# A new hand-written order of all tasks in a fused attention and feed-forward kernel

## The chip, the core and the metric

The kernel runs on one core of one Trainium2 chip. The metric is device time of one execution in microseconds (us). The core has five engines with a queue of their own each: TensorE (PE, with its weight loads shown as PEld), VectorE (DVE), ScalarE (ACT), GpSimd (POOL) and SyncE (SP), which here only issues DMAs. Each engine takes its instructions strictly in the order in which the program holds them, and they wait for each other through semaphores.

## The reference

The input x has 2048 tokens of 512 features. Two branches read it, and a gate of one value per token mixes them:

```python
q, k, v = x @ wq, x @ wk, x @ wv             # 32 heads of 16, four segments of 512 tokens
for s in range(4):                           # memory attention, branch A
    p = softmax(qs @ ks.T * scale + mask)    # causal within the segment
    a_dot = p @ vs
    a_mem = (phi(qs) @ M) / (phi(qs) @ z + 1e-6)      # phi(t) = t + 1 if t > 0 else exp(t)
    o = sigmoid(beta) * a_mem + (1 - sigmoid(beta)) * a_dot
    M, z = M + phi(ks).T @ vs, z + phi(ks).sum(0)
a = concat(o) @ wo
b = (gelu(x @ w_gate) * (x @ w_up)) @ w_down # branch B, 1792 hidden features
g = sigmoid((x * gate_w).sum(-1))
out = g * a + (1 - g) * b
```

## The kernel before

Everything is in bf16 with sums in f32. x is kept transposed in SBUF (xT: four chunks of 128 features by 2048 tokens), the weights too. The work is cut into named tasks, each belonging to one engine. A task's function issues the instructions; the class `Sched` (lines 160 to 193) goes through the text `ORDER` (lines 32 to 144) word by word and calls them. So `ORDER` is the schedule of all five engines at once: an engine's queue is the sequence of its own tasks in that text. A word is a name, then after @ the engine (A, D, P for ACT, DVE, POOL) where a task may go to several, then after # the letters of the buffers that it takes.

The names that matter, with s for the segment and c for a block of eight heads:

- `q{s}.{c}`, `k{s}.{c}`, `v{s}.{kt}`, `up{s}.{h}`: projection groups on PE, 16 small matmuls each; `gt{s}.{h}` is a pair of gate groups. `e` ahead of the name is the task that empties the PSUM bank: copies on DVE or ACT, the gelu on ACT for `egt`, the product with the gelu on DVE for `eup`. There are two single banks ("gen") and three double ones ("lg").
- `lg{n}`, n from 0 to 79: a slot of logits on PE (line 643), into two lg banks; `ex{n}a`, `ex{n}b`: the exponentials on ACT (line 664); `as{n}a`, `as{n}b`: the causal masks on POOL (line 673). `pv{s}.{c}e` and `pv{s}.{c}o`: probabilities times v on PE (line 692), each reading the masks of three slots; `epv` transposes the result on DVE (line 710); then `r`, `rg`, `n`, `m`, `o` normalise, add the memory part and transpose back into xT.
- `Ek`, `Emk`, `Qk`, `phk` and the same with q: the feature map, an exponential on ACT, two elementwise steps on DVE and a sum on DVE or POOL (line 767). For k the sum goes to a buffer `pkT`, of which there is one; `pk{s}.{p}` then issues two DMA transposes on SP (line 796) from pkT to `pk`, which `M{s}.{p}` multiplies with v on PE (line 808).
- `ko{s}.{c}`: a copy of k with every other head kept (line 406), on DVE or POOL. `den`, `num`, `rma`, `rmr`, `rmg`, `nm`: the memory read-out.
- `z{s}.{kt}`: the gate's products on DVE (line 525), 16 of them, from copies of x that lie in the buffers of `wdn` and `wo`; `zsp`: copies of their sums on POOL (line 536). Only when these are read can the SP tasks `wdn` and `wo` load the weights into the same buffers. `wos0` to `wos3` scale wo in place.
- `lx2`, `lx3`: SP loads segments 2 and 3 of x by four DMA transposes each (line 290); segment 1 and all other loads are issued ahead of the ordered part (lines 306 to 322).
- `dn{s}.{qt}.{h}` and `wo{s}.{qt}.{c}`: the output groups on PE; `os`, `st`: the scaled copy and the store of 128 rows. The last group is cut in two halves (`3.3h0`, `3.3h1`).

What orders the SP queue around the change is the place of its words among the others:

```python
    TAB["wo"] = add("wo", "SP", lambda _: load_w(nc.sync, wo, A_wo), kind="wol",
                    deps=zs[3 * KT:])
    a_x = [None, ext("x1")] + [add(f"lx{s}", "SP", lambda _, s=s: load_x(s), kind="lx")
                               for s in range(2, NSEG)]
```

Of the kernel before, what the change touches and what calls it, by code (L numbers as in the profile page):

```python
# [35 lines left out]
k0f3.1 q0.0#aa ek0.3@A ek0.0@D ek0.2@D gt0.1#b ko0.0@P#a Ek0.1#a ek0.1@A gt0.0#a Emk0.1 ko0.1@D  # L36
Qk0.1#a ko0.2@D#b ko0.3@D q0.1#b phk0.1@D#a egt0.0#a gt0.5#c eq0.1@D eq0.0@A egt0.1#b q0.2#ab
egt0.5#c lg0#ab eq0.2@D v0.1#b gt0.3#c ex0a#a Ek0.0#a q1.0#ac pk0.1#a ex0b#b gt1.4#a eq1.0@D z0.0
gt0.2#b Qk0.0#a egt1.4#d z0.3 ev0.1@D egt0.3#e Emk0.0 up0.3#a phk0.0@P#a egt0.2#f v0.3#b eup0.3
lg1#ac ev0.3@D up0.1#a as0a z2.1 ex1a#c v0.0#b eup0.1 ex1b#d as1a lg2#ba ev0.0@D v1.2#a as0b z1.0  # L40
ex2a#e q1.1#b ev1.2@D ex2b#f as2a lg3#cb eq1.1@D v1.0#a as1b tb ex3a#g as2b up0.5#b ev1.0@D ex3b#h
z3.3 lg4#ac v0.2#a ex4a#i eup0.5 omg v1.3#b ex4b#j as4a eb lg5#ba Eq1.0#a ev0.2@D as4b gt0.4#c
ev1.3@D as3a ex5a#k as3b Emq1.0 z3.1 ex5b#l pv0.0e#aa z2.0 gt1.1#b Qq1.0#a z1.3 epv0.0e gt0.6#a
egt0.4#g z3.0 egt1.1#h z0.2 pv0.0o#b bde0@D z3.2 egt0.6#i k1.0#ac epv0.0o wo lg6#cb lx3 ek1.0@D
up1.8#b ex6b#a up0.11#a eup1.8 ex6a#b lg7#ab eup0.11 k1.1#b ex7a#c as6a q0.3#a ek1.1@D as5a ex7b#d
bde3@D lg8#ca phq1.0@D#a M0.1#b ex8a#e gt1.5#b z1.1 lx2 r0.0#a Ek1.0#a z1.2 z0.1 gt1.2#c ex8b#f
eq0.3@D eM0.1 z2.3 gt1.3#a z2.2 egt1.5#j ko1.0@D#c zsp2 Qk1.0#a Emk1.0 egt1.2#k gt1.6#b pk0.0#b
as8b as7b egt1.3#l as5b as6b up0.7#a egt1.6#m as7a up0.13#b eup0.7 zsp1 lg9#ca eup0.13 zsp0
pv0.1e#ab ex9b#g phk1.0@D#a q1.2#ba epv0.1e pk1.0#a ex9a#h as9b lg10#ba eq1.2@D k2.0#aa as8a
ex10a#i ko1.1@P up1.9#b ek2.0@D ex10b#j wdn lg11#cb eup1.9 v1.1#a as9a ex11a#a bde2@P pv0.1o#b  # L50
as10b ex11b#b ev1.1@D as11a lg12#ac epv0.1o up0.12#a ex12a#k zsp3 r0.1#b q1.3#b eup0.12 ex12b#l
lg13#ba eq1.3@D g2 up1.7#a ex13b#c M0.0#b ex13a#d lg14#ca as13b eM0.0 rg0.1 up0.4#b as11b eup1.7
ex14b#e as12b up1.2#a eup0.4 as10a ex14a#f as13a lg15#ba eup1.2 bde1@P up0.6#b ex15b#g as14b
n0.1#a gt2.2#c ex15a#h as15b eup0.6 as12a Eq1.1#a as14a up0.10#a Qq1.1#a gt1.0#a eup0.10 wos1@D
egt2.2#n mbd0.1 Emq1.1 omz pv0.2e#bb egt1.0#o up1.3#a epv0.2e phq1.1@D#b lg16#bc up0.2#b eup1.3
ex16a#a zbd0 up1.5#a rg0.0 mbd0.2 mbd0.0 eup0.2 ex16b#b lg17#ab eup1.5 k2.1#b ex17b#i pv0.2o#a
ek2.1@D ex17a#j lg18#cb epv0.2o up0.8#b ex18b#c r0.2#b rg0.2 M1.0#a ex18a#d eM1.0 lg19#ab eup0.8
q2.0#ab n0.2#b ex19a#e up1.12#b wos0@D eq2.0@D ex19b#f as19a lg20#ca as17b den1#aa ex20a#k gt2.0#b
eden1 eup1.12 ex20b#l as20a as16a gt2.1#c as15a rma1.0#a egt2.0#p gt2.3#a as18a egt2.1#q as17a
as16b up1.6#a as18b egt2.3#r rma1.2 pv0.3e#bb eup1.6 lg21#bc epv0.3e up1.11#a as19b ex21b#a wos3@P  # L60
up0.9#b eup1.11 ex21a#b lg22#ac eup0.9 up1.10#a as21b ex22b#g as20b pv0.3o#b eup1.10 rma1.1
ex22a#h lg23#bc epv0.3o up1.1#a ex23b#c as22b k1.2#bb eup1.1 as22a ex23a#d mbd0.3 lg24#ac rma1.3
ek1.2@D k1.3#a ex24b#e up0.0#b ek1.3@D ex24a#f as24b lg25#bc as23b o0.2 Ek1.1#a num1.0#aa as23a
gt2.5#a eup0.0 as21a ex25a#i n0.0#b as24a Qk1.1#a ex25b#j pv1.0e#ba ko1.2@P#a gt2.6#b rmr1 o0.0
Emk1.1 egt2.5#s gt2.4#c r0.3#b enum1.0 egt2.6#t epv1.0e phk1.1@D#a pv1.0o#a egt2.4#u up1.4#b rg0.3
pk1.1#b epv1.0o lg26#ab eup1.4 v2.2#a n0.3#b ex26b#a q2.1#b ev2.2@D ex26a#b rmg1 lg27#cb eq2.1@D
up2.10#a ex27b#k as26a up2.13#b eup2.10 ex27a#l as27b r1.0#a lg28#ab rg1.0 ko1.3@P v2.0#a eup2.13
ex28b#c o0.3 up1.13#b ex28a#d ev2.0@D lg29#cb eup1.13 Eq2.0#a up2.2#a as28a as28b as27a ex29a#e
up2.4#b eup2.2 as25b as26b ex29b#f lg30#ac eup2.4 up2.5#a as25a Qq2.0#a ex30b#g as29b pv1.1e#bb
eup2.5 as29a ex30a#h lg31#bc epv1.1e as30b up2.3#a ex31b#a pv1.1o#b eup2.3 ex31a#b lg32#ac epv1.1o  # L70
up2.7#a ex32b#i n1.0#b up2.8#b mbd1.0 eup2.7 ex32a#j as32b lg33#bc eup2.8 up2.11#a as31b ex33b#c
nm1.0@D#a as32a k2.2#bc ex33a#d eup2.11 as31a lg34#ac ek2.2@D num1.1#aa ex34b#e as33b enum1.1
v2.1#b as33a ex34a#f as34b lg35#bc ev2.1@D up2.1#a as30a ex35b#k as34a o0.1 pv1.2e#ba nm1.1@P#b
eup2.1 ex35a#l lg36#ac epv1.2e pv1.2o#a wos2@P ex36b#a up2.0#b epv1.2o ex36a#b lg37#bc eup2.0
k2.3#a ex37b#g Emq2.0 phq2.0@D#c up1.0#b ex37a#h as37b ek2.3@D lg38#ac m1.0@P eup1.0 q3.0#ac
ex38b#c r1.1#b mbd1.1 q3.1#b rg1.1 ex38a#d eq3.0@D as38b as36a r1.2#a lg39#bc eq3.1@A rg1.2
dn0.3.0#a as35a dn0.3.1 ex39b#e as36b dn0.3.2 dn0.3.3 v2.3#b as37a Ek2.0#a as39b dn0.3.4 dn0.3.5
ev2.3@D dn0.3.6 as35b ex39a#f dn0.3.7 Qk2.0#a lg40#ac n1.2#a dn0.3.8 ex40b#i dn0.3.9 dn0.3.10
Emk2.0 num1.2#ba phk2.0@D#a dn0.3.11 dn0.3.12 ex40a#j dn0.3.13 as40b enum1.2 wo0.3.0 pk2.0#a
wo0.3.1 as39a wo0.3.2 o1.0 wo0.3.3 pv1.3e#ba as38a os0.3@A#a ko2.0@D#b lg41#bc epv1.3e pv1.3o#a  # L80
ex41a#a up2.9#b epv1.3o ex41b#b as41a r1.3#a lg42#ab eup2.9 nm1.2@P#c q2.2#aa ex42b#k M1.1#b as40a
eq2.2@A lg43#cb eM1.1 Eq3.0#a num1.3#ba dn0.0.0#a dn0.0.1 enum1.3 dn0.0.2 dn0.0.3 ex43b#l dn0.0.4
Qq3.0#a dn0.0.5 Emq3.0 q2.3#b rg1.3 ex43a#c m1.2@D mbd1.3 dn0.0.6 o1.2 dn0.0.7 ex42a#d dn0.0.8
dn0.0.9 nm1.3@D#a lg44#bc dn0.0.10 eq2.3@D ex44a#e dn0.0.11 dn0.0.12 dn0.0.13 phq3.0@D#a dn0.2.0#b
ex44b#f wo0.0.0 n1.3#b lg45#ab dn0.2.1 m1.3@D wo0.0.1 Eq2.1#a dn0.2.2 o1.3 wo0.0.2 wo0.0.3 gt3.4#c
zbd1 ex45a#g os0.0@D#b Emq2.1 st0.0 ex45b#h Qq2.1#a phq2.1@D#b dn0.2.3 dn0.2.4 dn0.2.5 as45b
dn0.2.6 dn0.2.7 as43a dn0.1.0#a as42a dn0.1.1 dn0.2.8 dn0.2.9 egt3.4#a as41b dn0.2.10 dn0.2.11
dn0.2.12 as42b dn0.2.13 wo0.2.0 wo0.2.1 as44b wo0.2.2 wo0.2.3 as45a lg46#ab os0.2@D#c ko2.1@P
Ek2.1#a dn0.1.2 dn0.1.3 pv2.0e#ba Qk2.1#a gt3.0#c ex46a#a as44a epv2.0e Emk2.1 as46a M2.0#b
dn0.1.4 as43b dn0.1.5 eM2.0 phk2.1@D#a dn0.1.6 egt3.0#b den2#ba dn0.1.7 mbd1.2 dn0.1.8 pk2.1#b  # L90
eden2 dn0.1.9 dn0.1.10 dn0.1.11 ko2.2@D#c dn0.1.12 rma2.0#a dn0.1.13 n1.1#a wo0.1.0 wo0.1.1
wo0.1.2 ex46b#b ko2.3@D wo0.1.3 lg47#ac os0.1@D#d rma2.3 pv2.0o#b ex47a#i m1.1@D k3.0#ab st0.1
epv2.0o ex47b#j as47a lg48#ba ek3.0@D v3.0#b rma2.1 ex48b#c dn1.3.0#a dn1.3.1 ev3.0@D ex48a#d
lg49#ca as47b dn1.3.2 M2.1#b ex49a#e as46b dn1.3.3 dn1.3.4 eM2.1 r2.0#a rma2.2 pv2.1e#bb ex49b#f
lg50#bc epv2.1e dn1.3.5 ex50a#k dn1.3.6 as49b dn1.3.7 rmr2 dn1.3.8 dn1.3.9 as48b num2.1#ba ex50b#l
as49a lg51#ab enum2.1 dn1.3.10 as48a dn1.3.11 ex51a#a mbd2.1 dn1.3.12 dn1.3.13 rmg2 wo1.3.0 o1.1
nm2.1@P#c pv2.1o#b ex51b#b lg52#ca epv2.1o wo1.3.1 ex52b#g wo1.3.2 wo1.3.3 q3.2#bb os1.3@D#b
ex52a#h r2.1#b lg53#ba st1.3 eq3.2@D num2.0#aa ex53a#c st0.3 gt3.5#c enum2.0 st0.2 ex53b#d
nm2.0@D#a num2.3#ba lg54#ba enum2.3 up2.6#a ex54a#e rg2.1 n2.1#b k3.1#b ex54b#f mbd2.0 m2.1@P
eup2.6 gt3.6#b ek3.1@D as54a as52b egt3.5#f k3.2#aa as53a as51b up3.8#b egt3.6#e ek3.2@D as52a  # L100
# [939 lines left out]
```

## Time and profile before

| | |
|---|---|
| median of three runs | 277.04 us (277.0 to 278.11) |
| the profiled execution's own time | 279.19 us |
| its span, first to last instruction | 277.5 us |
| mean granted TensorE clock in it | 0.994 |
| busy share PE, ACT, DVE, POOL | 96%, 82%, 65%, 51% |
| bytes moved by DMA | 15.83 MB |

The page shows one execution. Its second part cuts the span into 40 equal slices of 6.9 us and gives each engine's busy share in tenths. A group row gives line, engine, operation, names and shape, the count, then busy us and the mean ns of one, then the idle time before them and who ended it. A row of the waits reads: engine and line that waited, the one that it waited for, us in total, times, longest. A row of a timeline or of the chain begins with the start in us and the duration; in brackets stands the idle time before it.

### The profile page before, as it was taken

The numbers are of one execution on the slowest core, as the hardware profiler recorded it, in microseconds if no ns is written. First come the engines' busy times: TensorE is split into PE (matmuls) and PEld (weight loads), VectorE is DVE, ScalarE is ACT, GpSimd is POOL, SyncE is SP. The second block draws the span as 40 slices with busy tenths as digits, with TensorE's granted clock in tenths as the row PEclk, the third lists the DMA queues.
The fourth block names the chain that finished last, engine by engine and source line by source line (L and its number), as shares of the span: only waits on it lengthen the run. The fifth ranks groups of instructions, "written<-read, shape, count | busy, mean of one in ns | idle before, by whom it ended". The sixth has DMA issues, their size and how long they took to land.

```text
span 277.5 us, 11576 instructions
## 1 busy us (share of the span) xinstructions
PE 266.9 (96%) x5219; PEld 132.7 (48%) x5220; DVE 180.1 (65%) x355; ACT 228.6 (82%) x261; POOL 140.9 (51%) x264
## 2 busy tenths in 40 slices
PE   8999999978999999999999999999999999999993
...
ACT  2589999993999999999999999989998999970000
...
PEclk9999999997999999999999999999999999999999
...
GB/s 223 361 254 306 55 4 100 95 79 169 138 2 2 2 2 5 40 4 2 2 2 41 21 2 59 6 59 2 2 2 4 2 2 2 40 6 2 78 21 79
DMA packets 23539, 15.83 MB, mean 57 GB/s; under 512 B 13761, under 2 KB 22465, under 8 KB 23489
## 3 DMA queue, kind: packets, MB, share of 16 engines
...
q8 instruction: 41, 0.67, 1.1%
...
q14 instruction: 10, 0.07, 0.1%
HBM read 9.84 MB, written 2.10 MB: 43 GB/s over the span
## 4 chain that ended last, share of the span: by engine, by line
PE 78%; DMA 6%; DVE 6%; SPq 4%; POOL 3%; issue 1%; ACT 0%; ACTq 0%; DVEq 0%; POOLq 0%
PE dn L377 22%; PE up L377 17%; PE gt L377 11%; PE lg L643 8%; PE pv L692 6%; PE v L377 5%; PE k L377 4%; SPq L290 3%; PE q L377 3%; DMA wdn<-in_gate_w_dram 3%; POOL pT L673 2%; DVE wdn L525 2%; POOL rm L873 1%; DMA wdn<-in_A_x_dram 1%; PE num L377 1%
## 5 line engine op out<-in xcount | busy, mean ns | idle before, releaser
L230 ACT ACTIVATE pT<-lg 128x1024 bf16<-128x1024 f32 x160 | 152.4, 1028 | 10.5 <-PE lg L643 9.3
L673 POOL TENSOR_SCALAR_AFFINE_SELECT pT<-pT 128x512 bf16<-128x512 bf16 (+1 forms) x160 | 85.2, 564 | 72.1 <-ACT pT L230 68.4
L377 PE MATMUL dn<-wdn,G 128*32 128x512 bf16 (+1 forms) x952 | 60.2, 367 | 0.1
L377 PE MATMUL up<-xT,wup 128*32 128x512 bf16 x896 | 57.4, 384 | 0.0
L573 DVE TENSOR_TENSOR G<-up,G 128x512 bf16<-128x512 f32 x56 | 38.4, 687 | 22.7 <-PE up L377 22.4
L377 PE MATMUL gt<-xT,wga 128*32 128x512 bf16 x800 | 46.0, 379 | 0.0
L377 PEld LDWEIGHTS <-G 128*32 128x32 bf16 x952 | 24.0, 96 | 21.0 <-issue 2.4
L377 PEld LDWEIGHTS <-wup 128*32 128x32 bf16 x896 | 22.6, 97 | 22.4 <-issue 4.3
L710 DVE STREAM_TRANSPOSE T<-pv 128x512 f32<-128x512 f32 x32 | 22.6, 709 | 15.1 <-PE pv L692 14.7
L377 PEld LDWEIGHTS <-wga 128*32 128x32 bf16 x800 | 21.7, 97 | 19.8 <-issue 0.4
L230 ACT ACTIVATE G<-gt 128x1024 bf16<-128x1024 f32 x28 | 27.4, 1017 | 1.5 <-PE gt L373 0.9
L228 ACT ACT_TABLE_LOAD x22 | 28.2, 1283 | 0.4
L692 PE MATMUL pv<-pT,vz 128*32 128x256 bf16 (+2 forms) x640 | 23.2, 273 | 0.4 <-POOL pT L673 0.4
L948 ACT ACTIVATE osb<-dn,omz 128x512 bf16<-128x512 f32 (+1 forms) x3 | 1.8, 616 | 24.0 <-PE dn L377 24.0
L692 PEld LDWEIGHTS <-vz 128*32 128x32 bf16 x640 | 14.9, 97 | 10.9 <-issue 1.2
L377 PE MATMUL dn<-wo,xT 128*32 128x512 bf16 (+1 forms) x272 | 19.3, 367 | 0.0
L377 PEld LDWEIGHTS <-xT 128*32 128x32 bf16 x528 | 12.8, 96 | 13.3 <-issue 3.3
L950 DVE TENSOR_SCALAR osb<-dn,omz 128x512 bf16<-128x512 f32 (+1 forms) x14 | 10.2, 727 | 12.3 <-PE dn L377 12.1
L643 PE MATMUL lg<-qT,kO 32*128 32x128 bf16 (+2 forms) x320 | 17.6, 272 | 0.0
L643 PE MATMUL lg<-qT,kT 16*128 16x256 bf16 (+2 forms) x320 | 17.5, 273 | 0.0
L377 PE MATMUL v<-wv,xT 128*32 128x512 bf16 x256 | 16.6, 381 | 0.8 <-DVE vz L236 0.6
L873 POOL TENSOR_SCALAR rm<-Tm 32x32 f32<-32x32 f32 x48 | 14.6, 304 | 4.9 <-DVE Tm L867 1.7
...
## 6 DMA issues: line engine op xcount, KB each, us to landing
...
```

What stands on the lines that cost most here:

```text
L228: nc.scalar.activation(nil[0][:, 1:2], nil[0][:, 0:1], func)
L230: nc.scalar.activation(dst, src, func, **kw)
L290: nc.sync.dma_start_transpose(xT[:, fc, s * L:(s + 1) * L], x2[s * L:(s + 1) * L, fc * P:(fc + 1) * P])
L377: nc.tensor.matmul(out[a], lhsT=lhsT[:, a], rhs=rhs, start=start, stop=stop, tile_position=(0, 32 * j), skip_group_check=True)
L525: nc.vector.scalar_tensor_tensor(out=xr[s][:, kt, :], in0=xr[s][:, kt, :], scalar=1.0, in1=gwb, op0=ALU.mult, op1=ALU.mult, accum_out=zc[: ...
L573: UPT[(s, hs)] = evac("DVE", g, box, lambda e, t: nc.vector.tensor_mul(G[(s, hs // 2)][:, hs % 2, :], t[:, :], G[(s, hs // 2)][:, hs % 2, ...
L643: nc.tensor.matmul(A[j // 2][:, j % 2, at * P:(at + nq) * P], lhsT=l, rhs=r, start=True, stop=True, tile_position=(32 * j, 0))
L673: nc.gpsimd.affine_select(out=v, in_=v, pattern=pat, compare_op=ALU.is_ge, fill=0.0, base=0, channel_multiplier=-1)
L692: nc.tensor.matmul(t[32 * j:32 * j + 32, qb * P:(qb + nq) * P], lhsT=vz[s % 2][:, kt, h * VW:h * VW + 32], rhs=pT[(s, t0 + w, j // 2)][:, ...
L710: nc.vector.transpose(TT[key][:, e, :, :].rearrange("p a b -> p (a b)"), t[:, :])
L873: eng_of[e].tensor_scalar_add(RMt[s][32 * j:32 * j + 32, c, :, :], bx["Td"][32 * c:32 * c + 32, :, 2 * j:2 * j + 2], 1e-6)
L950: nc.vector.tensor_scalar_mul(bx["o"][:, lo:hi], box["t"][:, 0:hi - lo], g)
```

## The change

Only the text `ORDER` is replaced from its fourth line on; no function changes. The same tasks are called in another sequence, some on another engine, some with other buffer letters. On SP the tasks stand as follows:

```
before: pk0.1 wo lx3 lx2 pk0.0 pk1.0 wdn pk1.1 pk2.0 st0.0 pk2.1 st0.1 st1.3 st0.3 st0.2 st1.2 ...
after:  pk0.0 lx2 pk0.1 pk1.0 lx3 wo pk1.1 wdn pk2.0 st0.3 pk2.1 st0.1 st1.3 st1.1 st1.0 st0.0 ...
```

Tasks by engine, where one can be chosen:

| | before | after |
|---|---|---|
| odd copies `ko` on POOL | 6 of 16 | 9 of 16 |
| feature sums `phk`, `phq` on POOL | 1 and 1 | 3 and 1 |
| memory products `nm` on POOL | 7 of 12 | 9 of 12 |
| `bde`, `wos` on POOL | 2 and 2 | 1 and 1 |
| copies `ek`, `eq`, `ev` on ACT | 3, 3, 0 | 5, 3, 1 |
| output copies `os` on ACT | 3 of 17 | 6 of 17 |
| changes between gelu and exponentials on ACT | 22 | 20 |

The core of the diff, the stretch from the first q group to lg9 (the rest is of the same kind):

```diff
-k0f3.1 q0.0#aa ek0.3@A ek0.0@D ek0.2@D gt0.1#b ko0.0@P#a Ek0.1#a ek0.1@A gt0.0#a Emk0.1 ko0.1@D
-Qk0.1#a ko0.2@D#b ko0.3@D q0.1#b phk0.1@D#a egt0.0#a gt0.5#c eq0.1@D eq0.0@A egt0.1#b q0.2#ab
-egt0.5#c lg0#ab eq0.2@D v0.1#b gt0.3#c ex0a#a Ek0.0#a q1.0#ac pk0.1#a ex0b#b gt1.4#a eq1.0@D z0.0
-gt0.2#b Qk0.0#a egt1.4#d z0.3 ev0.1@D egt0.3#e Emk0.0 up0.3#a phk0.0@P#a egt0.2#f v0.3#b eup0.3
...
-egt0.4#g z3.0 egt1.1#h z0.2 pv0.0o#b bde0@D z3.2 egt0.6#i k1.0#ac epv0.0o wo lg6#cb lx3 ek1.0@D
-up1.8#b ex6b#a up0.11#a eup1.8 ex6a#b lg7#ab eup0.11 k1.1#b ex7a#c as6a q0.3#a ek1.1@D as5a ex7b#d
-bde3@D lg8#ca phq1.0@D#a M0.1#b ex8a#e gt1.5#b z1.1 lx2 r0.0#a Ek1.0#a z1.2 z0.1 gt1.2#c ex8b#f
-eq0.3@D eM0.1 z2.3 gt1.3#a z2.2 egt1.5#j ko1.0@D#c zsp2 Qk1.0#a Emk1.0 egt1.2#k gt1.6#b pk0.0#b
-as8b as7b egt1.3#l as5b as6b up0.7#a egt1.6#m as7a up0.13#b eup0.7 zsp1 lg9#ca eup0.13 zsp0
-pv0.1e#ab ex9b#g phk1.0@D#a q1.2#ba epv0.1e pk1.0#a ex9a#h as9b lg10#ba eq1.2@D k2.0#aa as8a
...
+k0f3.1 q0.0#aa ek0.3@A ek0.0@D ek0.1@A gt0.1#b ko0.0@P#a ek0.2@A Ek0.0#a gt0.0#c Emk0.0 Qk0.0#a
+phk0.0@P#a egt0.1#a v0.1#b egt0.0#b gt0.2#a ev0.1@D ko0.2@P#b eq0.0@A lg0#bc egt0.2#c q0.1#b
+ko0.1@P v0.3#a eq0.1@D ko0.3@P gt0.5#a ev0.3@D ex0a#a Ek0.1#a q0.2#bb pk0.0#a ex0b#b gt1.4#b
+eq0.2@D gt0.3#c egt0.5#d egt1.4#e z0.3 q1.0#ac z0.1 egt0.3#f v1.0#b lx2 eq1.0@D lg1#ab ev1.0@D
+v1.2#a z1.3 ex1a#c up0.3#b ev1.2@D ex1b#d as1a lg2#ca eup0.3 up1.8#a Emk0.1 ex2b#e as1b q1.1#b
+eup1.8 tb ex2a#f as2b lg3#ba eq1.1@D up0.11#a ex3a#g Qk0.1#a phk0.1@D#a v0.0#b ex3b#h eup0.11
+pk0.1#b lg4#cb ev0.0@D v0.2#a ex4b#i up0.7#b ex4a#j ev0.2@D as4b lg5#ab as2a eup0.7 Eq1.0#a
+gt1.1#c as0a as3b ex5a#k as4a as0b M0.0#a ex5b#l as5a gt0.4#a eM0.0 as3a z1.0 Qq1.0#a M0.1#b
+gt0.6#b egt1.1#g eM0.1 Emq1.0 omg phq1.0@D#a pv0.0e#aa z1.1 egt0.6#i up0.5#b epv0.0e eb
+lg6#ca eup0.5 k1.0#ac ex6a#a k1.1#b ek1.0@D ex6b#b as6a lg7#bc ek1.1@D v1.1#a as5b bde1@D ex7a#c
+as6b up0.1#b ev1.1@D bde2@P ex7b#d z2.0 lg8#ab pv0.0o#a Ek1.0#a z3.1 gt1.3#c z2.1 ex8b#e epv0.0o
+ex8a#f r0.0#a gt1.6#b z0.0 z2.3 mbd0.1 z1.2 gt1.5#a egt1.6#j z3.0 eup0.1 egt1.3#k gt1.2#b Emk1.0
+z3.3 egt1.5#l z2.2 z3.2 up0.13#a egt1.2#m z0.2 up0.4#b eup0.13 zsp2 lg9#ca eup0.4 k2.0#aa as7a
+ex9b#g as8a up1.11#b ek2.0@D as7b ex9a#h as8b lg10#ba eup1.11 zsp0 q1.2#aa ex10a#i bde3@D zbd0
+Qk1.0#a pv0.1e#bb as9b ex10b#j eq1.2@D lg11#cb zsp3 epv0.1e up1.9#a ex11a#a as9a ex11b#b eup1.9
+lg12#ac zsp1 pv0.1o#b phk1.0@D#a ex12b#k up1.2#a epv0.1o as11a pk1.0#a ex12a#l r0.1#b lg13#bc
...
```

In the next stretches pk1.0 is followed by lx3 and wo between lg13 and lg16; the part around pv0.3e, and the end, read:

```diff
+lg17#ac eup0.2 up0.6#a ex17a#i rg0.2 as16b up1.1#b eup0.6 rma1.1 ex17b#j lg18#ba eup1.1 up1.3#a
+ex18a#c as15b up1.12#b rma1.2 eup1.3 ex18b#d lg19#cb eup1.12 k1.2#ab ex19a#e n0.2#b k1.3#b mbd0.2
+ex19b#f lg20#ac ek1.3@D gt2.0#b as19b ex20a#k rmr1 as18b as18a ex20b#l as17a gt2.1#a as19a as20a
+as17b egt2.0#p num1.0#ba wos2@P gt2.3#c enum1.0 egt2.1#q ek1.2@D as16a rmg1 k2.1#b egt2.3#r rg0.0
+ko1.2@D#b nm1.0@P#a pv0.3e#ab ek2.1@D lg21#ba epv0.3e up0.8#b ex21a#a up1.6#a eup0.8 ex21b#b as21a
...
+pv3.3o#a os2.1@A#c dn3.3h0.11 dn3.3h0.12 dn3.1.3 epv3.3o num3.2#ba st2.1 dn3.2.8 st1.2 dn3.1.4
+r3.3#a dn3.1.5 o3.1 dn3.1.6 dn3.1.7 dn3.1.8 n3.2#b dn3.1.9 dn3.1.10 dn3.1.11 o3.0 dn3.1.12
...
+os3.3h0@A#b dn3.0.13 wo3.0.0 dn3.3h1.0#c wo3.2.0 wo3.2.1 dn3.3h1.1 dn3.3h1.2 dn3.3h1.3 dn3.3h1.4
+dn3.3h1.5 wo3.2.2 wo3.2.3 dn3.3h1.6 dn3.3h1.7 dn3.3h1.8 os3.2@A#a wo3.1.3 wo3.0.1 wo3.0.2
+os3.1@D#c wo3.0.3 st3.2 dn3.3h1.9 dn3.3h1.10 st3.3h0 dn3.3h1.11 os3.0@D#d dn3.3h1.12 dn3.3h1.13
+wo3.3h1.0 st3.1 wo3.3h1.1 wo3.3h1.2 wo3.3h1.3 st3.0 os3.3h1@A st3.3h1
```

215 lines of the change are left out of this document (107 added, 108 removed).

## Prediction

> **What bounds the kernel now.** I read the page first, then the stretches in which TensorE stood still, then who was waited for, then the queue behind that wait.
>
> ```profile
> span 277.5 us, 11576 instructions
> PE 266.9 (96%) x5219; PEld 132.7 (48%) x5220; DVE 180.1 (65%) x355; ACT 228.6 (82%) x261; POOL 140.9 (51%) x264
> PE   8999999978999999999999999999999999999993
> ACT  2589999993999999999999999989998999970000
> PEclk9999999997999999999999999999999999999999
> ```
>
> TensorE is busy 96% of the span. Beside start and end there is one dent, in slices 9 and 10 (55 to 69 us), and the granted clock dips there too. The windows cut it out, with a stretch of the steady part below; columns are busy us and instructions of PE, PEld, DVE, ACT, POOL, then the clock.
>
> ```profile
> 60.00:63.20 3.20, 0.55 (x8) 0.22 (x5) 1.37 (x3) 2.85 (x4) 2.96 (x4) 0.98 0.22 44
> 63.20:66.66 3.46, 3.46 (x33) 1.24 (x33) 1.22 (x2) 0.00 (x0) 1.13 (x3) 0.52 0.40 84
> 100.00:120.00 20.00, 20.00 (x404) 9.41 (x396) 16.92 (x31) 19.77 (x24) 11.76 (x21) 1.00 0.08 16
> ```
>
> PE stops for 2.65 us of the first stretch, and in the next it issues at clock 0.52: 3.46 x 0.48 = 1.66 us lost. In the steady part PE has no idle time and ACT has 1%: there the order can win nothing, only lose. The waits and the chain say who is late:
>
> ```profile
> DVE pkT L767 <- DMA pk<-pkT: 2.8, 1, 2.8
> PE k L377 <- DVE T L710: 2.7, 1, 2.7
> PE v L377 <- DVE vz L236: 0.6, 1, 0.6
> PE gt L373 <- DMA wga<-in_B_w_gate_dram: 0.5, 1, 0.5
> ```
> ```profile
> 59.19 2.47 DMA pk<-pkT
> 61.83 0.69 DVE pkT L767
> 62.52 0.64 DVE T L710
> 63.20 1.90 PE k L377 x13
> ```
>
> Read backwards: k2.0 waits for a PSUM bank that epv0.1e empties; that DVE transpose stands behind phk1.0, which writes the only pkT buffer and so waits until pk0.0 has read it, at 61.66. The SP queue tells why pk0.0 is so late:
>
> ```profile
> 19.94 2.02 SPq L322 DMA_DIRECT2D beta<-in_A_beta_dram  x1
> 22.08 5.18 SPq L796 DMA_TRANSPOSE pk<-pkT  x2
> 44.16 0.37 SPq L295 DMA_DIRECT2D wo<-in_A_wo_dram  x1
> 44.57 12.43 SPq L290 DMA_TRANSPOSE xT<-in_A_x_dram  x8
> 57.10 7.99 SPq L796 DMA_TRANSPOSE pk<-pkT  x4
> 65.13 0.58 SPq L295 DMA_DIRECT2D wdn<-in_B_w_down_dram  x1
> ```
>
> SP stands from 27.3 to 44.2 in front of the wo load, which waits for the z products that read wo's buffer. Then eight x transposes take 12.43 us of issue, and pk0.0 comes ninth.
>
> **The change, part by part.** The tasks are the same; only their places, some engines and buffers move.
>
> *SP.* The order pk0.1, wo, lx3, lx2, pk0.0, pk1.0, wdn, pk1.1 becomes pk0.0, lx2, pk0.1, pk1.0, lx3, wo, pk1.1, wdn. pk0.0 can start where pk0.1 did: 22.08 to 27.3. lx2, four transposes, needs nothing; at 12.43 / 8 = 1.55 us each it ends at 33.5. If the start-up loads slow it, two in 5.18 us make 10.4 and the end 37.7; this is the far bound. pk0.1 then needs phk0.1, which stands on DVE behind q1.1's copy just ahead of lg3. These rows place it and its reader M0.1:
>
> ```profile
> 36.95 0.39 PE L643 MATMUL lg<-qT,kT 16*128 16x512 bf16 x4
> 29.62 0.86 PE v L377 x16
> 76.03 1.73 PE gt L377 x32
> 39.19 0.55 PE pv L692 x20
> L767 DVE TENSOR_TENSOR pkT<-E,Q x5: 647/684/692, 14.1 to 166.3; 128x1024 bf16<-128x1024 bf16 x5
> DMA to landing us min/median/max: 2.4/2.5/9.0
> ```
>
> A projection group is 0.86 us, a gate pair 1.73, a logit slot 0.39, a pv 0.55; a change between logits and the rest costs about 0.1 more. Up to lg5 both orders hold the same PE tasks but one or two, so lg5 stays near 36.95. Two groups and a slot per step put lg3 near 32.6; copy, maximum and sum on DVE (0.68 each at most) make phk0.1 ready at 34.6, and pk0.1, half of 7.99 us of issue, lands at 34.6 + 4.0 + 1.2 = 39.8. Behind lg5 PE runs gt1.1, M0.0 and gt0.4 before M0.1: 36.95 + 0.5 + 1.73 + 0.4 + 1.73 = 41.3. There are 1.5 us to spare, so I price it at 0. By the far bound pk0.1 starts at 37.7 and lands at 42.9: 1.6 us of wait.
>
> So pkT is free at 40, and phk1.0, after lg12, finds it empty: the **2.65 us** go, and with them what they do to the clock, **1.70 us** (1.66, and 0.02 x 3.2 before 63.2). The wo load loses its early place, behind lx3; its first reader is wos2 on POOL after lg20, some 20 us later, so nothing waits. wdn is read first by dn0.3.0 after lg40; again nothing.
>
> *The opening.* The 0.5 us wait for the gate weights stays: gt0.2 needs the same load. The 0.6 us wait of v0.3 for DVE goes, since z0.0 and z0.3 no longer stand in front of ev0.1 and ev0.3:
>
> ```profile
> 27.26 1.05 PE L377 MATMUL v<-wv,xT 128*32 128x512 bf16 x16 [0.57 <-DVE vz L236]
> L230 ACT ACTIVATE pT<-lg 128x1024 bf16<-128x1024 f32 x160 | 152.4, 1028 | 10.5 <-PE lg L643 9.3 <-POOL kO L406 0.3
> L228 ACT ACT_TABLE_LOAD x22 | 28.2, 1283 | 0.4
> ```
>
> But ek0.2 moves to ACT ahead of Ek0.0, and ACT starts ex1a some 0.3 us later. Bounds 0 and -0.57; I take **-0.4**. Table loads fall from 22 to 20 (2 x 1.28 = 2.6 us). Eight copies come to ACT and two leave it; four of the eight stand behind the last exponential, where ACT is idle (the last slices of its row), the others weigh no more than the loads saved. PE, busy throughout, covers both: 0.
>
> *POOL.* Three odd copies, two feature sums and two Nm products come to POOL, one wo scaling and one bde leave it.
>
> ```profile
> L406 POOL TENSOR_SCALAR kO<-kT,odd 128x512 bf16<-128x512 bf16 x6 | 9.6, 1592 | 3.9 <-DVE kT L236 3.9
> L767 POOL TENSOR_TENSOR pkT<-E,Q 128x1024 bf16<-128x1024 bf16 x1 | 2.3, 2264 | 19.3 <-DMA pk<-pkT 19.3
> L591 POOL TENSOR_SCALAR wo<-wo,omg 128x512 bf16<-128x512 bf16 x2 | 3.1, 1568 | 0.0
> L673 POOL TENSOR_SCALAR_AFFINE_SELECT pT<-pT 128x512 bf16<-128x512 bf16 x96 | 61.3, 656 | 51.4 <-ACT pT L230 47.9 <-PE lg L643 2.8
> L673 POOL TENSOR_SCALAR_AFFINE_SELECT pT<-pT 128x256 bf16<-128x256 bf16 x64 | 26.7, 427 | 20.8 <-ACT pT L230 20.4
> ```
>
> That is 3 x 1.59 + 2 x 2.26 and two products of 1 to 1.6, less 1.57 and 0.6: some 9 to 10 us on an engine busy 51%. The tightest place I found is **pv0.3e**, which needs as16a. From ex19b on POOL does as19b, as18b, as18a, as17a, as19a, as20a, as17b, wos2, as16a: five masks at 0.656, three at 0.427, one scaling at 1.57, 6.1 us in all, beginning 2.4 us after lg19 (slot and two exponentials): 8.5. PE from lg19: two slots, k1.2, k1.3, gt2.0, gt2.1, num1.0, gt2.3, k2.1 = 0.8 + 2.6 + 5.2 + 0.2 and 0.4 of changes = 9.2. It fits by 0.7 us; bounds 0 and 3.6 (below). I take **+0.2** for this and other small new waits.
>
> *The end.* After pv3.3o DVE must give T, r, N, Nm, the sums and four xT transposes before wo3.3h0.3. In the old order such a row of work took
>
> ```profile
> 258.04:266.00 7.96, 7.28 (x14) 1.00 0.16 51
> ```
>
> 7.3 us; the new one has 13 of these. PE has meanwhile 31 whole and 6 half steps, 31 x 0.216 + 6 x 0.108 + 0.2 = 7.6 us. Bounds 0 and 0.6; I take 0. The last matmul, copy and store are the same.
>
> **Sum**, against the profiled execution's own 279.19 us (span 277.5 and 1.7 around it): 279.19 - 2.65 - 1.70 - 0.4 + 0.2 = 274.6. The runs shown have a median of 277.04 (277.0 to 278.11), 2.15 less. I read this so that most of them have the gap but not the dip: 279.19 - 1.70 = 277.5, near the median. Then 277.04 - 2.65 - 0.4 + 0.2 = 274.2. Between the two I predict **274.4 us**.
>
> The Trainium skill, TensorE: Matmul & The Clock Gate, "What's actually happening", says that the clock halves after at least one idle window of about 3.4 us, and that the windows run freely. Here a stop of 2.65 us sufficed, so the trace shows that a window need not be idle throughout; where it falls still changes from run to run. By the page's letter no run would pay the dip (274.2); paid by all, it would be 272.5.
>
> **The rivals.**
> - *B, the dip is in the ordinary runs too*: 277.04 - 4.35 - 0.4 + 0.2 = 272.5. For it: the profiled one has it. Against: the 2.15 us between profile and median.
> - *C, M0.1 waits instead*: lx2 is slowed by the start-up loads, as pk0.1 was (5.18 us for two). 1.6 us by the far bound, 274.4 + 1.6 = 276.0. Against: by 27.3 most of the loads have landed.
> - *D, the stop moves to pv0.1e*, so the change does not do what it says. zsp2 on POOL waits for the last z product and stands in front of the masks as7a to as8b. Behind epv0.0o DVE now has eight z products and five other instructions:
>
> ```profile
> L525 DVE SCALAR_TENSOR_TENSOR wdn<-wdn 128x512 bf16<-128x512 bf16 x12 | 8.0, 678 | 1.8 <-DMA wdn<-in_gate_w_dram 1.8
> L536 POOL COPY G<-zc 32x16 f32<-32x16 f32 x16 | 3.5, 219 | 5.8 <-DVE wdn L525 5.1
> ```
>
>   8 x 0.68 + 2.5 + 4 copies (0.9) + three masks (1.7) = 10.5 us; PE needs four gate pairs, five groups and two slots, 12.4. It fits by 1.9; if not, a stop like the old one: 274.4 + 2.65 = 277.0.
> - *E, slower: POOL is late at pv0.3e.* The masks there can be longer than their means:
>
> ```profile
> L673 POOL TENSOR_SCALAR_AFFINE_SELECT pT<-pT x160: 403/636/1099, 33.8 to 253.7; 128x512 bf16<-128x512 bf16 x96, 128x256 bf16<-128x256 bf16 x64
> ```
>
>   All eight at 1.099 add 5 x 0.44 + 3 x 0.67 = 4.2 us and stop PE for 3.6 with the 0.7 used up; such a stop brings the half clock again, 1.7: 274.4 + 5.3 = 279.7. It decides from a stop of 2.3 us on (274.4 + 2.3 + 1.7 = 278.4). Against: the median is 0.64, and in the old order pv0.3e never stopped PE, though behind a shorter queue (some 7 us of POOL work since lg16 against 12 now). The Trainium skill, GPSIMD Engine Reference, "Key points", says that GpSimd shares its SBUF interfaces with VectorE and contends with it in some DVE modes; the spread 403 to 1099 agrees with that, and by that rule E is the danger of more work on POOL.
>
> **How the numbers follow.** Forecast 0.56 (its own range 273.2 to 275.6), B 0.14, C 0.07, D 0.08, E 0.15. This measurement tells 0.5%, 1.4 us, from no change: 275.65 and 278.43. Faster: forecast, B and a little of C, 0.71; same: the rest of C and D, 0.14; slower: E, 0.15. The range 272.0 to 277.8 takes in B, C and D and leaves out E and the lowest part of B.
>
> **What would show it.** Right: no PE gap above 1 us between 20 and 270 us; the clock at 9 in slice 10; no DVE wait on pk<-pkT; on SP, x transposes at about 27 to 34, the next pk pair near 35, the wo load after 65; 20 table loads; POOL near 150 us with PE still at 267 or less. Wrong: PE idle before M (L808) near 41 us (C), before pv near 63 (D) or near 90 (E), or waits of 0.5 us in many places, which would mean an order too tight for what its steps really take.

## Result, and the profile after

| | before | after |
|---|---|---|
| median | 277.02 us (276.5 to 278.11) | 273.94 us (273.88 to 274.31) |
| ratio of the two | | 0.9887 (95%: 0.9856 to 0.9917) |
| the profiled execution's own time | 279.19 us | 274.31 us |
| its span, mean granted clock | 277.5 us, 0.994 | 272.6 us, 0.998 |
| last matmul ends, rest of the span | 273.12, 4.35 us | 267.65, 4.94 us |

The new order is faster by 3.1 us, 1.1%; 274.4 us were forecast. Ratios, here and below, leave out the slowest executions (in the experiments 10 of the 55 of the order before, all at a granted clock of 0.994 or less), so a ratio need not be the quotient of the two medians beside it. The page after, with the span, the busy shares and the slices of PE and of its clock:

```profile
span 272.6 us, 11613 instructions
PE 265.0 (97%) x5232; PEld 132.2 (48%) x5232; DVE 174.8 (64%) x344; ACT 228.2 (84%) x263; POOL 148.2 (54%) x269
PE   7999999999999999999999999999999999999992
PEclk9999999999999999999999999999999999999999
```

The dent in PE's row and the dip in the clock's row, slices 9 and 10 before, are both gone. The windows say how much each stretch gave: busy us of PE, PEld, DVE, ACT, POOL, then clock, DMA share, GB/s. First the order before, then the one after:

```profile
0.00:20.00 20.00, 17.69 (x139) 11.35 (x144) 6.85 (x17) 10.87 (x16) 7.38 (x16) 1.00 0.99 274
20.00:60.00 40.00, 39.43 (x790) 19.03 (x780) 28.93 (x70) 39.07 (x46) 14.06 (x30) 1.00 0.53 116
60.00:70.00 10.00, 7.35 (x120) 3.24 (x120) 5.00 (x9) 5.70 (x8) 5.57 (x11) 0.83 0.55 154
70.00:240.00 170.00, 169.27 (x3480) 81.03 (x3472) 120.66 (x230) 163.75 (x185) 100.25 (x182) 1.00 0.06 17
240.00:277.50 37.50, 33.12 (x720) 18.08 (x708) 18.69 (x31) 9.22 (x11) 13.62 (x26) 1.00 0.11 35
```
```profile
0.00:20.00 20.00, 17.99 (x156) 11.43 (x160) 4.95 (x13) 11.35 (x17) 13.49 (x20) 1.00 0.99 271
20.00:60.00 40.00, 40.00 (x820) 19.31 (x812) 29.25 (x71) 39.23 (x47) 11.23 (x25) 1.00 0.48 94
60.00:70.00 10.00, 9.64 (x200) 4.37 (x200) 8.32 (x15) 9.84 (x13) 9.29 (x23) 1.00 0.27 31
70.00:240.00 170.00, 169.70 (x3480) 81.55 (x3476) 120.10 (x226) 160.29 (x180) 106.37 (x193) 1.00 0.11 29
240.00:272.60 32.60, 27.65 (x600) 15.53 (x596) 12.16 (x22) 7.49 (x10) 7.84 (x12) 0.98 0.13 43
```

The stretch less PE's busy time is PE's idle time. Up to 240 us it was 2.31 + 0.57 + 2.65 + 0.73 = 6.26 us and is 2.01 + 0 + 0.36 + 0.30 = 2.67; behind 240 us PE works without a break to its last matmul in both (the clock of 0.98 in the last row comes from the 1.3 us from 271.3 on, when PE is done). Busy time fell from 266.86 to 264.98 us. Of these 1.88 us, 1.69 are the time lost at half clock (4.34 by b_pk0 below, less the stop of 2.65). The rest belongs to the opening: two groups overlap by 0.18 us when PE does not stop between them, and b_z2 below puts the opening at 0.75 and not 0.57. So the two profiled executions divide like this (us):

| term | predicted | measured |
|---|---|---|
| the stop at 60 to 63 us | -2.65 | -2.65 |
| half clock behind it | -1.70 | -1.69 |
| the opening: 20 to 60 us | -0.4 | -0.57 - 0.18 = -0.75 |
| the start-up: 0 to 20 us | | -0.30 |
| other waits of PE | +0.2 | +0.36 - 0.43 = -0.07 |
| behind the last matmul | 0 | +0.59 |
| sum | -4.55 | -4.87 |

The SP queue of the order after:

```profile
21.52 5.34 SPq L796 DMA_TRANSPOSE pk<-pkT  x2
26.91 7.82 SPq L290 DMA_TRANSPOSE xT<-in_A_x_dram  x4
34.83 32.62 SPq L796 DMA_TRANSPOSE pk<-pkT  x4
67.50 6.21 SPq L290 DMA_TRANSPOSE xT<-in_A_x_dram  x4
73.75 0.58 SPq L295 DMA_DIRECT2D wo<-in_A_wo_dram  x1
```

pk0.0 stands at 21.5, lx2 behind it, pk0.1 at 34.8 (its row also takes in pk1.0 at 64.95, and SP's wait between them), the wo load at 73.75. This is the order that was drawn in advance. TensorE around the two places where a new wait could have come, M0.1 and pv0.1e:

```profile
38.44 1.92 PE L377 MATMUL gt<-xT,wga 128*32 128x512 bf16 x32
40.18 0.42 PE L808 MATMUL M<-vz,pk 128*32 128x34 bf16 x32
...
61.05 0.72 PE L692 MATMUL pv<-pT,vz 128*32 128x512 bf16 x20
61.70 0.40 PE L643 MATMUL lg<-qT,kT 16*128 16x256 bf16 x12
62.46 1.05 PE L377 MATMUL up<-xT,wup 128*32 128x512 bf16 x16 [0.36 <-DVE qT L236]
```

Neither waits. But the second transfer of pk0.1 landed at 40.10, and M0.1 began at 40.18: 0.08 us to spare. In the four other profiles of this order and its small variants below it landed between 37.51 and 39.92, with 0.25 (a_tail), 0.69 (a_both), 2.75 (after_again) and 2.76 us (a_eq) to spare. The only stop of this stretch is a small one behind lg11, for the bank that eq1.2 empties. (In the new order's line above that begins `gt0.6#b egt1.1#g` the word `egt0.4#h` stands behind `omg`.)

### The profile page after: what moved, and what is told of

Same layout as the page of the kernel before. It is cut to its first block, busy times and chain, and to the rows that moved or that the text cites. A ratio compares the mean times of both kernels' runs of the same rounds, so it can differ in the third digit from the quotient of the medians.

```text
span 272.6 us, 11613 instructions
## 1 busy us (share of the span) xinstructions
PE 265.0 (97%) x5232; PEld 132.2 (48%) x5232; DVE 174.8 (64%) x344; ACT 228.2 (84%) x263; POOL 148.2 (54%) x269
## 4 chain that ended last, share of the span: by engine, by line
PE 94%; DMA 2%; DVE 1%; ACT 0%; issue 0%; SPq 0%; DVEq 0%
PE dn L377 24%; PE up L377 19%; PE gt L377 16%; PE lg L643 9%; PE pv L692 7%; PE v L377 5%; PE q L377 5%; PE k L377 4%; PE gt L373 2%; DMA wk<-in_A_wk_dram 2%; PE k L373 1%; PE num L377 1%; PE M L808 1%; PE q L373 0%; PE v L373 0%; DVE Q L760 0%
## 5 line engine op out<-in xcount | busy, mean ns | idle before, releaser
L673 POOL TENSOR_SCALAR_AFFINE_SELECT pT<-pT 128x512 bf16<-128x512 bf16 (+1 forms) x160 | 84.3, 555 | 68.9 <-ACT pT L230 67.7
L377 PE MATMUL dn<-wdn,G 128*32 128x512 bf16 (+1 forms) x952 | 59.1, 367 | 0.0
L377 PE MATMUL up<-xT,wup 128*32 128x512 bf16 x896 | 56.3, 380 | 0.4 <-DVE qT L236 0.4
L948 ACT ACTIVATE osb<-dn,omz 128x512 bf16<-128x512 f32 (+1 forms) x6 | 3.7, 616 | 22.7 <-PE dn L377 22.7
L692 PEld LDWEIGHTS <-vz 128*32 128x32 bf16 x640 | 14.0, 97 | 9.9 <-issue 1.5
L873 POOL TENSOR_SCALAR rm<-Tm 32x32 f32<-32x32 f32 x48 | 13.7, 286 | 8.0 <-ACT G L230 4.8
L950 DVE TENSOR_SCALAR osb<-dn,omz 128x512 bf16<-128x512 f32 x11 | 8.0, 736 | 14.9 <-PE dn L377 14.7
L406 POOL TENSOR_SCALAR kO<-kT,odd 128x512 bf16<-128x512 bf16 x9 | 14.0, 1562 | 4.3 <-DVE kT L236 4.3
```

Source lines behind the costliest of these rows:

```text
L377: nc.tensor.matmul(out[a], lhsT=lhsT[:, a], rhs=rhs, start=start, stop=stop, tile_position=(0, 32 * j), skip_group_check=True)
L406: eng_of[e].tensor_scalar_mul(QK[ko][:, c % 2, :], QK[("k", s, pr)][:, c % 2, :], odd[:, :])
L673: nc.gpsimd.affine_select(out=v, in_=v, pattern=pat, compare_op=ALU.is_ge, fill=0.0, base=0, channel_multiplier=-1)
L692: nc.tensor.matmul(t[32 * j:32 * j + 32, qb * P:(qb + nq) * P], lhsT=vz[s % 2][:, kt, h * VW:h * VW + 32], rhs=pT[(s, t0 + w, j // 2)][:, ...
L873: eng_of[e].tensor_scalar_add(RMt[s][32 * j:32 * j + 32, c, :, :], bx["Td"][32 * c:32 * c + 32, :, 2 * j:2 * j + 2], 1e-6)
L950: nc.vector.tensor_scalar_mul(bx["o"][:, lo:hi], box["t"][:, 0:hi - lo], g)
```

## The experiments

Each kernel is one of the two orders with words of `ORDER` moved. Medians are compared with the order before, run on the same chip.

| kernel | median, us (executions) | order before there | ratio (95%) |
|---|---|---|---|
| b_pk0 | 274.77 (12) | 277.51 | 0.9923 (0.9893 to 0.9954) |
| b_pk0_z | 276.05 (12) | 277.51 | 0.9963 (0.994 to 0.9985) |
| a_lx3 | 279.86 (8) | 277.51 | 1.0086 (1.0039 to 1.0132) |
| after_again | 274.45 (6) | 276.88 | 0.9885 (0.9837 to 0.9932) |
| a_tail | 273.34 (6) | 276.88 | 0.9863 (0.9818 to 0.9908) |
| a_eq | 274.12 (6) | 276.88 | 0.9884 (0.9841 to 0.9927) |
| a_both | 273.89 (6) | 276.88 | 0.9874 (0.9832 to 0.9917) |
| b_pk0_2 | 274.46 (12) | 277.81 | 0.991 (0.9871 to 0.9948) |
| b_z2 | 274.14 (6) | 277.81 | 0.9894 (0.9831 to 0.9957) |

**b_pk0: the order before with one word moved.**

```diff
-gt0.2#b Qk0.0#a egt1.4#d z0.3 ev0.1@D egt0.3#e Emk0.0 up0.3#a phk0.0@P#a egt0.2#f v0.3#b eup0.3
+gt0.2#b Qk0.0#a egt1.4#d z0.3 ev0.1@D egt0.3#e Emk0.0 up0.3#a phk0.0@P#a pk0.0#b egt0.2#f v0.3#b eup0.3
...
-eq0.3@D eM0.1 z2.3 gt1.3#a z2.2 egt1.5#j ko1.0@D#c zsp2 Qk1.0#a Emk1.0 egt1.2#k gt1.6#b pk0.0#b
+eq0.3@D eM0.1 z2.3 gt1.3#a z2.2 egt1.5#j ko1.0@D#c zsp2 Qk1.0#a Emk1.0 egt1.2#k gt1.6#b
```

> The order of before with one word moved: pk0.0 stands right behind phk0.0, ahead of wo, lx3 and lx2 on SP; no other engine's queue changes. Theory (the place of pk0.0 on SP alone makes the stop near 60 us): pk0.0 is issued near 34 us, the DVE wait on pk<-pkT and the PE gap of 2.65 us are gone, and with them the half clock; ordinary runs 277.0 - 2.65 = 274.4, ratio 0.990. Rival 1 (the gain comes from the rest of the new order): 276.3 or more, ratio above 0.997. Rival 2 (k2.0 then waits for segment 2 of x, which landed at 59.65): a PE gap of up to 1 us stays, 275.4.

TensorE of b_pk0 in the stretch where the order before stands still:

```profile
61.29 0.42 PE L643 MATMUL lg<-qT,kT 16*128 16x512 bf16 x4
61.64 1.05 PE L377 MATMUL k<-xT,wk 128*32 128x512 bf16 x16
62.52 1.04 PE L377 MATMUL up<-xT,wup 128*32 128x512 bf16 x16
63.49 0.40 PE L643 MATMUL lg<-qT,kT 16*128 16x256 bf16 x12
```

From lg10 to lg11 it takes 63.49 - 61.29 = 2.20 us; the order before took 66.66 - 60.12 = 6.54. k2.0 follows at once and lasts 1.05, not 1.90: stop and half clock are gone together, 4.34 us, against the 4.35 of the prediction. One word in another place removes the stop, with the rest of the order as it was, so rival 1 is out. pk0.0 is issued at 32.43. Rival 2 is out as well: the last part of segment 2 landed at 60.49, and k2.0 began at 61.64.

**b_pk0_z: the same, and z0.0 and z0.3 put behind ev0.3.**

```diff
-egt0.5#c lg0#ab eq0.2@D v0.1#b gt0.3#c ex0a#a Ek0.0#a q1.0#ac pk0.1#a ex0b#b gt1.4#a eq1.0@D z0.0
-gt0.2#b Qk0.0#a egt1.4#d z0.3 ev0.1@D egt0.3#e Emk0.0 up0.3#a phk0.0@P#a pk0.0#b egt0.2#f v0.3#b eup0.3
-lg1#ac ev0.3@D up0.1#a as0a z2.1 ex1a#c v0.0#b eup0.1 ex1b#d as1a lg2#ba ev0.0@D v1.2#a as0b z1.0
+egt0.5#c lg0#ab eq0.2@D v0.1#b gt0.3#c ex0a#a Ek0.0#a q1.0#ac pk0.1#a ex0b#b gt1.4#a eq1.0@D
+gt0.2#b Qk0.0#a egt1.4#d ev0.1@D egt0.3#e Emk0.0 up0.3#a phk0.0@P#a pk0.0#b egt0.2#f v0.3#b eup0.3
+lg1#ac ev0.3@D z0.0 z0.3 up0.1#a as0a z2.1 ex1a#c v0.0#b eup0.1 ex1b#d as1a lg2#ba ev0.0@D v1.2#a as0b z1.0
```

> The same, and z0.0 and z0.3 behind ev0.3 on DVE. Theory (in the opening ev0.1 stands behind z0.0, which waits for the late landing of gate_w at 24.94, and so v0.3 waits 0.6 us): the wait of v0.3 goes and lg1 starts 0.6 to 0.85 us earlier, 0.6 to 0.85 us less than with pk0.0 alone, about 273.7. Rival (ACT sets the pace of the opening, as the prediction had it in part): lg1 earlier, but ex1a is not, and at most 0.3 us come through to the end.

It lost 1.3 us against b_pk0 where it should have gained. TensorE of b_pk0_z behind lg1 shows two new stops:

```profile
31.11 1.05 PE L377 MATMUL v<-wv,xT 128*32 128x512 bf16 x16 [0.69 <-DVE G L573]
...
34.17 1.05 PE L377 MATMUL v<-wv,xT 128*32 128x512 bf16 x16 [0.82 <-DVE vz L236]
```

The first is my own doing: at 28.55 to 30.4 DVE has z0.0, z0.3 and z2.1 one behind the other, and eup0.1 comes after them. The second is not, as b_pk0_2 below shows.

**a_lx3: the new order with lx3 ahead of pk0.1**, so that eight x transposes stand in front of it rather than four.

```diff
-pk0.1#b lg4#cb ev0.0@D v0.2#a ex4b#i up0.7#b ex4a#j ev0.2@D as4b lg5#ab as2a eup0.7 Eq1.0#a
+lx3 pk0.1#b lg4#cb ev0.0@D v0.2#a ex4b#i up0.7#b ex4a#j ev0.2@D as4b lg5#ab as2a eup0.7 Eq1.0#a
...
-as12b eup1.2 q0.3#b as10a ex13a#c as10b up1.10#a ko2.0@P#c eq0.3@D ex13b#d lx3 lg14#ab eup1.10
+as12b eup1.2 q0.3#b as10a ex13a#c as10b up1.10#a ko2.0@P#c eq0.3@D ex13b#d lg14#ab eup1.10
```

> The order of after with one word moved: lx3 stands ahead of pk0.1 on SP. Theory (a feature map's DMA transposes that come late on SP stop PE by their whole delay, and the half clock follows a long stop): four more x transposes of 1.26 to 1.95 us each put pk0.1 5 to 6.2 us later; it landed at 40.10 and M0.1 began at 40.18, so PE stops for 5 to 6.2 us before M0.1, and then loses 1.7 us more at half clock; 273.9 + 5 to 7.9 = 279 to 281.8. Rival (the stop is made up later, since ACT, DVE and POOL run ahead in it): less than 3 us are left at the end, below 277.

SP and TensorE of a_lx3, and its window from 36 to 50 us (columns as above):

```profile
27.78 12.28 SPq L290 DMA_TRANSPOSE xT<-in_A_x_dram  x8
40.16 2.53 SPq L796 DMA_TRANSPOSE pk<-pkT  x2
```
```profile
42.66 0.30 PE L808 MATMUL M<-vz,pk 128*32 128x34 bf16 x16 [2.48 <-DMA pk<-pkT]
43.95 0.31 PE L808 MATMUL M<-vz,pk 128*32 128x34 bf16 x16 [0.99 <-DMA pk<-pkT]
44.09 3.59 PE L377 MATMUL gt<-xT,wga 128*32 128x512 bf16 x32
```
```profile
36.00:50.00 14.00, 10.54 (x211) 4.92 (x212) 5.17 (x17) 8.48 (x10) 2.90 (x7) 0.76 0.34 59
```

pk0.1 is issued 5.3 us later than in the order after, PE stands for 14.00 - 10.54 = 3.46 us, and the gate pair behind it takes 3.59 us, not 1.92. From lg5 to lg6 it is 13.89 us where the order after has 7.56: 6.33 more, of which 2.87 are the half clock. The last matmul is 6.3 us later against lg0: nothing is made up. The stop is shorter than the 5 to 6.2 us expected, since the second transfer of pk0.1 landed 2.5 us after its issue here (41.42 to 43.91) and took 4.0 in the order after (36.09 to 40.10): it is 3.81 us later, not 5.3. The loss is as large all the same, since the half clock stayed for two windows of 3.41 us here. One of the eight executions, of 276.92 us, had a granted clock of 0.997, as if it had the stop alone. Where four loads stand in this queue decides 6 us in the median.

**after_again, a_tail, a_eq, a_both: the new order again, with one or two small moves.** a_tail issues the store st3.3h0 as soon as its data are there; a_eq lets DVE empty q1.2's bank before it does Qk1.0; a_both does both.

```diff
-os3.3h0@A#b dn3.0.13 wo3.0.0 dn3.3h1.0#c wo3.2.0 wo3.2.1 dn3.3h1.1 dn3.3h1.2 dn3.3h1.3 dn3.3h1.4
+os3.3h0@A#b st3.3h0 dn3.0.13 wo3.0.0 dn3.3h1.0#c wo3.2.0 wo3.2.1 dn3.3h1.1 dn3.3h1.2 dn3.3h1.3 dn3.3h1.4
...
-os3.1@D#c wo3.0.3 st3.2 dn3.3h1.9 dn3.3h1.10 st3.3h0 dn3.3h1.11 os3.0@D#d dn3.3h1.12 dn3.3h1.13
+os3.1@D#c wo3.0.3 st3.2 dn3.3h1.9 dn3.3h1.10 dn3.3h1.11 os3.0@D#d dn3.3h1.12 dn3.3h1.13
```
```diff
-Qk1.0#a pv0.1e#bb as9b ex10b#j eq1.2@D lg11#cb zsp3 epv0.1e up1.9#a ex11a#a as9a ex11b#b eup1.9
+eq1.2@D Qk1.0#a pv0.1e#bb as9b ex10b#j lg11#cb zsp3 epv0.1e up1.9#a ex11a#a as9a ex11b#b eup1.9
```

> The changed order once more, on the same chip as the three kernels below, for a closer ratio. From its first runs 273.9 us, ratio 0.9885. The move of pk0.0 alone gave 0.9923 (0.9893 to 0.9954). Theory (pk0.0's place carries the main part, the rest of the new order under 1 us): ratio 0.987 to 0.991. Rival (the rest of the order is worth as much as that place, some 2.5 us): ratio at or below 0.984. The half clock behind x's stop is absent in every execution: granted clock 0.996 or more throughout.

0.9885 again, beside 0.9923 and 0.991 for pk0.0's move alone: by these values the place of one word carries most of the gain, though the intervals overlap, so how much the rest adds is not settled by times.

> The changed order with one move: the store st3.3h0 is issued right behind os3.3h0, whose copy ended at 263.63, rather than in the burst of five stores between 266.25 and 269.8. Theory (the last store is late because the issues ahead of it on SP take up to 1.75 us each): st3.3h1 is issued within 0.4 us of its data at 268.2, the span ends 0.6 us earlier against PE's end (0.4 to 1.2). Against the changed order: -0.6 us. Rival (the end is set by how fast the output's bytes drain, whenever they are issued): the distance from PE's end to the span's end stays at 4.9 us, 0 gained.

The end of the span: ACT's last copy and SP's stores, first in the order after (the second store of the five and the last one are shown), then in a_tail.

```profile
267.71 0.47 ACT L948 ACTIVATE osb<-dn,omz 128x256 bf16<-128x256 f32 x1 [1.49 <-PE dn L377]
```
```profile
266.63 1.75 SPq L919 DMA_DIRECT2D out_dram<-osb  x1
```
```profile
269.46 0.37 SPq L919 DMA_DIRECT2D out_dram<-osb  x1
```
```profile
266.97 0.47 ACT L948 ACTIVATE osb<-dn,omz 128x256 bf16<-128x256 f32 x1 [1.49 <-PE dn L377]
```
```profile
267.80 0.37 SPq L919 DMA_DIRECT2D out_dram<-osb  x1
```

In the order after the last store's data are there at 268.18 and it is issued at 269.46, 1.28 us late, because the store at 266.63 held SP for 1.75 us; in a_tail at 267.44 and 267.80, 0.36 late. From the last issue to the end of the span it is 3.12 to 3.14 us in the order after and in all four of these profiles, so the end is set by when that store is issued, not by how the output drains: the rival is out. From PE's end to the span's end there are 4.94, 5.27 and 4.49 us where the store is not moved (order after, after_again, a_eq), 4.02 and 4.35 where it is (a_tail, a_both): the means are some 0.7 us apart. The times bear it out as far as they go: the 12 executions with the move have a mean of 273.64, the 12 without it 274.12, 0.48 apart with 0.49 of uncertainty. a_tail, at 273.34, is the lowest median of all.

> The changed order with one move: eq1.2 goes on VectorE ahead of Qk1.0, which took 0.87 us; PE stood 0.36 us at 62.46 before up1.9 for the bank that eq1.2 empties. Theory: that stop goes and stays gone, -0.3 to -0.4 us from lg11 to the end. Rival: the same time is lost at the next step (Qk1.0 and its phk1.0 are later by eq1.2's duration, or PE waits for ScalarE's exponents): 0. A move of this size is at the edge of what five rounds can tell, so the trace decides: the gap at 62.5 and the distance from lg10 to lg20 (25.56 in the changed order).

The stop before up1.9 was gone, but in after_again it was gone too, with nothing moved. DVE and POOL in the order after as first profiled, then POOL and DVE in after_again:

```profile
60.94 0.87 DVE L760 TENSOR_SCALAR Q<-kT 128x1024 bf16<-128x1024 bf16 x1
```
```profile
60.90 0.63 POOL L673 TENSOR_SCALAR_AFFINE_SELECT pT<-pT 128x512 bf16<-128x512 bf16 x1
```
```profile
61.13 0.94 POOL L673 TENSOR_SCALAR_AFFINE_SELECT pT<-pT 128x512 bf16<-128x512 bf16 x1
```
```profile
61.16 0.42 DVE L760 TENSOR_SCALAR Q<-kT 128x1024 bf16<-128x1024 bf16 x1
```

In the first, a mask on POOL and Qk1.0 on DVE begin 0.04 us apart; the mask takes its usual 0.63 us and Qk1.0 takes 0.87. In after_again they begin 0.03 us apart (61.13 and 61.16); Qk1.0 takes 0.42 and the mask 0.94. Of the two one goes first, and the other waits. So the same program has this stop in some executions and not in others, and what a_eq's move does to it is not shown. With the stop lg10 to lg20 takes 25.56 us (25.57 in a_tail), without it 25.39 (25.38 in a_eq): it is worth 0.18 us, half of what I had put on it.

> Both moves above in one kernel, an attempt at an order better than the changed one. If the two stops are independent, the sum of both: -1.0 us against the changed order (272.9), ratio near 0.985. If only the first holds: 273.3. If both fell: as the changed order, 273.9.

273.89 us: a_tail's gain is inside the uncertainty here, and a_eq's cannot be seen.

**b_z2 and b_pk0_2: the opening.** b_z2 is b_pk0 with z0.0 behind ev0.1 and z0.3 behind Emk0.0; b_pk0_2 is b_pk0 once more.

```diff
-egt0.5#c lg0#ab eq0.2@D v0.1#b gt0.3#c ex0a#a Ek0.0#a q1.0#ac pk0.1#a ex0b#b gt1.4#a eq1.0@D z0.0
-gt0.2#b Qk0.0#a egt1.4#d z0.3 ev0.1@D egt0.3#e Emk0.0 up0.3#a phk0.0@P#a pk0.0#b egt0.2#f v0.3#b eup0.3
+egt0.5#c lg0#ab eq0.2@D v0.1#b gt0.3#c ex0a#a Ek0.0#a q1.0#ac pk0.1#a ex0b#b gt1.4#a eq1.0@D
+gt0.2#b Qk0.0#a egt1.4#d ev0.1@D z0.0 egt0.3#e Emk0.0 z0.3 up0.3#a phk0.0@P#a pk0.0#b egt0.2#f v0.3#b eup0.3
```

> The order before with pk0.0 right behind phk0.0, and the first two gate products on VectorE one step later each: z0.0 behind ev0.1 (no longer ahead of it) and z0.3 behind Emk0.0, in gaps that VectorE had there, so that no eviction after lg1 moves. Theory (the opening gained because ev0.1 stood behind z0.0, which waits for the gate weights' landing at 23.8 to 25.0): the stop before v0.3 goes, lg0 to lg1 takes 9.08 us where the order before took 9.82, and lg1 to lg5 stays at 9.19; against the next kernel 0 to -0.7 us, by how early the start-up work ends. Rival (the products cost the same wherever they stand, as where they stood behind ev0.3): lg1 to lg5 grows by 0.5 us or more, and the time is that of the next kernel or worse.

> The order before with pk0.0 right behind phk0.0 and nothing else, once more beside the kernel above. As measured first: ratio 0.992 (0.989 to 0.995), lg10 to lg11 in 2.2 us, granted clock of 0.996 or more in every execution. Theory on the opening: where the start-up ends early (lg0 before 18.5 us), lg0 to lg1 takes 9.8 us here; where it ends late (lg0 at 19.8 the first time), 9.08.

DVE in the order before, then in b_z2, both with lg0 at 18.42:

```profile
24.96 0.69 DVE L525 SCALAR_TENSOR_TENSOR wdn<-wdn 128x512 bf16<-128x512 bf16 x1 [1.84 <-DMA wdn<-in_gate_w_dram]
...
26.53 0.68 DVE L236 CAST vz<-v 128x512 bf16<-128x512 f32 x1
```
```profile
23.37 0.69 DVE L236 CAST vz<-v 128x512 bf16<-128x512 f32 x1
24.63 0.69 DVE L525 SCALAR_TENSOR_TENSOR wdn<-wdn 128x512 bf16<-128x512 bf16 x1 [0.57 <-DMA wdn<-in_gate_w_dram]
```

In the order before DVE waits 1.84 us for the gate weights and then does z0.0, Qk0.0 and z0.3 ahead of ev0.1, at 26.53. In b_z2 ev0.1 has gone at 23.37, and the same wait for a landing at nearly the same time holds up nobody: lg0 to lg1 takes 27.49 - 18.42 = 9.07 us where the order before took 28.24 - 18.42 = 9.82. That is 0.75 us for two words. b_pk0 and b_pk0_2 had no such wait in their profiles (lg0 only at 19.84 and 18.95, lg1 9.08 and 9.07 behind it): their gate weights were there in time. So of three profiles with the old opening only one has the stop; in how many executions it occurs is open, and the medians of b_z2 and b_pk0_2, 274.14 and 274.46, are too close to tell.

From lg1 to lg5 b_z2 took 8.97 us, less than the 9.19 expected but more than the 8.71 of the order before, so that 0.49 of its 0.75 us are left at lg5. b_pk0_2 did worse: 10.05. Its rows say why. POOL, DVE and PE of b_pk0_2, then POOL and DVE of b_z2:

```profile
30.23 2.13 POOL L767 TENSOR_TENSOR pkT<-E,Q 128x1024 bf16<-128x1024 bf16 x1 [16.80 <-DVE G L573]
```
```profile
30.92 1.99 DVE L525 SCALAR_TENSOR_TENSOR wdn<-wdn 128x512 bf16<-128x512 bf16 x1
```
```profile
33.58 1.05 PE L377 MATMUL v<-wv,xT 128*32 128x512 bf16 x16 [0.79 <-DVE vz L236]
```
```profile
31.74 2.12 POOL L767 TENSOR_TENSOR pkT<-E,Q 128x1024 bf16<-128x1024 bf16 x1 [19.03 <-DMA pk<-pkT]
```
```profile
30.39 0.68 DVE L525 SCALAR_TENSOR_TENSOR wdn<-wdn 128x512 bf16<-128x512 bf16 x1
```

z1.0 takes 0.68 us when POOL is idle, and 1.99 when it begins 0.69 us into phk0.0's 2.13 us on POOL: until POOL is done, and 0.55 us more. ev1.2, which stands behind it, comes late, and PE stands 0.79 us for the bank that it empties. This is the second stop of b_pk0_z as well (z1.0 there took 1.93). So the profiled execution of b_pk0_z loses by two causes: three products in a row, and a collision between two engines that the order of neither shows.

## Why the prediction was right, and where its terms were off

**The bound and the chain** were right, and the step is shown alone by b_pk0: pk0.0's place on SP, through the one pkT buffer, the transpose behind phk1.0 and the bank of k2.0. 2.65 us of stop and 1.70 of half clock were forecast, 4.34 measured. The median, 273.94 us, is 0.5 below the 274.4 forecast.

**From profile to median.** I read the 2.15 us between the profiled execution and the median as the half clock, present in that execution and absent in most. In the three comparisons of the experiments the order before ran 55 times: 19 times with a granted clock of 0.994 or less, with a median of 279.4 us, and 36 times with 0.996 or more, with a median of 276.9. The 70 executions of kernels with pk0.0 early, the order after among them and a_lx3 left out, had 0.996 or more throughout. So the median gains the stop, and the dip only in the share of executions that has it. Rival B, the dip in the ordinary executions too, is out. The two groups lie 2.5 us apart, though, and one window of 3.41 us at half clock costs 1.7; where the other 0.8 comes from, no trace here shows.

**The opening** was mis-sized: -0.4 was taken between bounds of 0 and -0.57, because ACT would start 0.3 us later. It is -0.75 by b_z2 beside the order before, and in the order after too: 9.94 us from lg0 to lg1, less 0.86 for the one projection group more that stands there, is 9.08 beside 9.82. The row that I took as the bound, 0.57 us of idle time before v0.3, leaves out the 0.18 us by which two groups overlap when PE runs on (a v group lasts 1.05 us and the next begins after 0.87). ACT's later start cost nothing that can be seen: PE has no idle time from 20 to 60 us.

**M0.1's spare time** was put at 1.5 us, and 0.08 are left in the order after as first profiled, 0.25 to 2.76 in the four other profiles. The times on SP came close to the forecast (pk0.1 issued at 34.83, 34.6 forecast; landed at 40.10, 39.8 forecast), but not by the steps that were summed. phk0.1 was done at 33.6, not 34.6, and pk0.1 stood behind lx2 on SP, which ended at 34.73, not 33.5. And the row `57.10 7.99`, half of which was taken for a pair's issue, holds a stand of SP between its two pairs:

```profile
57.10 3.36 SPq L796 DMA_TRANSPOSE pk<-pkT  x2
62.59 2.50 SPq L796 DMA_TRANSPOSE pk<-pkT  x2
```

The pair pk0.1 took 2.52 us of issue and not 4.0, and its second transfer landed 2.75 us behind the end of its issue and not 1.2. That these errors cancel is luck. PE was at M0.1 at 40.18 and not 41.3: lg5 came 0.8 earlier, mainly since the opening no longer stops, and the work from lg5 to M0.1 took 4.05 us where 4.36 were summed. Rival C was therefore near in that execution. Its price of 1.6 us leaves out the half clock: in a_lx3 3.46 us of standing at M0.1 cost 6.33. Whether a stop of 1.6 us would bring it, no run shows.

**pv0.1e (rival D) and pv0.3e (rival E).** Neither stops. The masks that pv0.1e reads were done by 59.9 and it began at 61.05, so 1.1 us were spare, where I had 1.9. For pv0.3e the POOL and PE rows of the order after are

```profile
89.20 1.56 POOL L591 TENSOR_SCALAR wo<-wo,omg 128x512 bf16<-128x512 bf16 x1
90.73 0.63 POOL L673 TENSOR_SCALAR_AFFINE_SELECT pT<-pT 128x512 bf16<-128x512 bf16 x1
```
```profile
91.14 1.04 PE L377 MATMUL k<-xT,wk 128*32 128x512 bf16 x16
92.01 0.72 PE L692 MATMUL pv<-pT,vz 128*32 128x512 bf16 x20
```

as16a is done at 91.36, pv0.3e begins at 92.01: 0.65 us to spare, 0.7 forecast. (In rival E, 4.2 less the 0.7 is 3.5 and not 3.6; nothing hangs on it.)

**Other waits** were put at +0.2 and came to -0.07. The 0.36 before up1.9 is what I had in mind; against it the waits from 70 to 240 us fell from 0.73 to 0.30 us.

**The end** was put at 0 with the reason that the last matmul, copy and store are the same. They are, but not what stands ahead of that store on SP: the failed step is that I counted the stores as free. a_tail and a_both show 0.7 us of it. (The 7.6 us of PE's work summed there is 7.54.) By the table the errors in the opening (-0.35), the start-up (-0.30), the half clock (+0.01), the other waits (-0.27) and the end (+0.59) leave -0.32. That the total is closer than its terms is luck: the end happens to cancel the others, and the start-up differs by more than this from one execution to the next.

**What the rest of the new order is worth.** From lg0 to the last matmul b_z2, the order before with three words moved, takes 250.02 us; the order after 250.19, but with q0.2's 0.86 us of work moved behind lg0, so 249.33. All its other moves gain 0.7 us on PE and give 0.6 back behind it (4.32 us in b_z2, 4.94 in the order after). Their times cannot be told apart: 0.9894 and 0.9885. What stays open is which of those moves gains the 0.7 us; that was not tried.
